# Turning the last tile of an attention unit on TensorE instead of by DMA

## Chip, cores and metric

The kernel runs on one core of a Trainium2 chip. The metric is the time of one execution in device microseconds; profiles come from single executions.

## What is computed

An attention with a learned bias on relative positions, then two feed-forward layers, each two matrix products with a function between them. Cut to what matters:

```python
B, H, S, D = 2, 8, 576, 64                       # q, k, v: (B, H, S, D)
scores = q @ k.transpose(0, 1, 3, 2) / np.sqrt(D)
x = log1p(abs(i - j)) / log1p(max(i, 1))         # one number for each pair of positions
bias = relu(x[..., None] @ w1 + b1) @ w2         # 32 hidden, one output for each head
attn = softmax(scores + bias)
y = (attn @ v).transpose(0, 2, 1, 3).reshape(1152, 512)
h = y @ moe_w_in                                 # (1152, 512) x (512, 2048)
g = (a0 + a1*h + a2*h**2 + a3*h**3) / (1 + abs(b0)*abs(h) + abs(b1)*h**2 + 1e-6)
y = g @ moe_w_out                                # (1152, 2048) x (2048, 512)
out = leaky_relu(y @ moe2_w_in, 0.01) @ moe2_w_out
```

## The kernel before

Four stages follow each other in one program. The engines' queues are in order, and the order in each is written out by hand: lists of pairs (step, operation) say at which step of a loop an operation is issued, and within a step the order of the list holds.

**Bias** (to about 76 us): the bias of all pairs is built and laid into `bias_m` and `bias_r` in SBUF.

**Attention** (about 76 to 237 us): a unit is a pair of heads of one batch entry; there are 8 units. A unit has 9 tiles of 128 rows x 576 columns: tiles 0 to 7 are four row blocks of either head, and the ninth (j = 8, tile (8, 2)) holds the last 64 rows of both heads. Step s of the loop belongs to tile s (9 steps a unit). For a tile:

- `qk` (L721): scores on TensorE in fp32r, six matmuls, issued one step ahead. Their PSUM pool has two buffers.
- `ttr` (L733): VectorE adds the bias and takes the row minimum, out of PSUM into `pt`.
- `exps` (L749): ScalarE takes the exponent into one of two `ex` buffers and sums the rows into `sums`.
- `hi`, one step later (L771 on ScalarE, L773 on VectorE, by the sets `HI_ACT`): the exponent is cast to fp16, first half of the buffer `hl`.
- `lo`, two steps later (L786): what the cast lost is put into the second half of `hl`. The first 512 columns go to GpSimd or, by `LO_DVE`, to VectorE; the last 64 to VectorE or, by `REM_POOL`, to GpSimd. The sets with `_END` hold for the last unit.
- When a group of tiles is complete in `hl` (two tiles, or the ninth alone: `GROUPS`), SyncE issues a DMA transpose into `et` (L792), where the columns lie on partitions. `hl` has three buffers.

Behind a unit come, by `PLAN` (steps count from the unit's first tile, so that step 9 is step 0 of the next unit): `rsum`, `rrec` (L819, L823: one over the row sums), `rbx` (L829, a product with the identity turns them; L832 copies it), `rbc` (L840, L842: spread over partitions), `av` with c = 0, 1, 2 (L813: attention times v, fp16, 28 matmuls each; c = 2 is the ninth tile), `rev` (L846), `rmul` (L855), `xhi`, `xlo` (L859, L864: the result split in two fp32r halves). Ahead of a unit come `load`, `prep_q`, `prep_ql`, `prep_k`, `v_sum`, `v_scale`, `prep_v8`, `prep_vd`. The outputs of `av` and of `rbx`/`rbc` share one PSUM tag, "v", with two buffers; `v_sum` and `v_scale` use spare columns of `rbc`'s.

`TAIL` is the same for the last two units (its first argument is 0 for the unit before the last, 1 for the last). In between stand the first operations of the next stage: the first weights (`w_load`, `w_dve`, `w_hi`, `w_lo`), the first product `gemm1` (L359, one call is nine matmuls of 384 columns, or three for one chunk) and the function on its result (`r_abs`, `r_s1` and so on). The first ones of `START` follow.

**First and second feed-forward layer** (to the end): products L359, L940 and L981 on TensorE, the rational function on VectorE, ScalarE and GpSimd (`plan_first` arranges the first layer, `PLAN2` the second).

Of the kernel before, what the change touches and what calls it, by code (L numbers as in the profile page):

```python
# [156 lines left out]
TAIL = [(2, 'rbx', 0), (3, 'rbc', 0), (2, 'w_load', -2, 0), (1, 'av', 0, 0, 0, 1), (0, 'rsum', 0),
        (0, 'rrec', 0), (8, 'w_dve', -2, 1, 0, 1), (18, 'w_lo', -2, 1), (7, 'av', 0, 1, 0, 1),
        (6, 'rmul', 0, 0), (5, 'w_dve', -2, 0, 0, 1), (8, 'w_load', -2, 1), (9, 'rsum', 1),
        (9, 'rrec', 1), (12, 'xhi', 0, 1), (12, 'open_h0'), (10, 'rbx', 1), (12, 'w_dve', -2, 1, 1, 2),  # L160
        (14, 'av', 1, 1, 0, 1), (7, 'av', 0, 2, 0, 1), (9, 'rmul', 0, 1), (9, 'w_dve', -2, 2, 0, 1),
        (11, 'w_dve', -2, 0, 1, 2), (12, 'rbc', 1), (9, 'xhi', 0, 0), (9, 'av', 1, 0, 0, 1),
        (10, 'w_hi', -2, 0), (21, 'w_dve', -1, 0, 1, 2), (15, 'av', 1, 2, 0, 1), (11, 'w_lo', -2, 0),
        (12, 'gemm1', 0, 0), (12, 'rev', 1), (12, 'rmul', 1, 0), (3, 'rev', 0),
        (12, 'w_dve', -2, 2, 1, 2), (14, 'w_load', -1, 0), (15, 'w_hi', -2, 1), (13, 'gemm1', 0, 2),
        (15, 'gemm1', 0, 3, (0,)), (16, 'w_dve', -1, 0, 0, 1), (21, 'w_hi', -1, 0), (21, 'r_s1', 0, 2),
# [1038 lines left out]
```

## Time and profile before

| | |
|---|---|
| median of 3 runs | 674.03 us (673.1 to 675.94) |
| profiled execution | 678.19 us, span of its instructions 676.4 us |
| TensorE busy | 598.4 us, 88% of the span |
| VectorE busy | 526.1 us, 78% |
| ScalarE busy | 410.2 us, 61% |
| GpSimd busy | 360.0 us, 53% |
| granted TensorE clock, mean | 0.959 |

All times of instructions are counted from the span's start. [...]

### The profile page before, as it was taken

What the parts mean: (1) busy time and instruction counts of PE and PEld (TensorE: products, weight loads), DVE (VectorE), ACT (ScalarE), POOL (GpSimd) and SP (SyncE); (2) the same over time, 40 slices, a digit from 0 to 9 for tenths busy, and PEclk for the clock granted to TensorE, in tenths of its full rate; (3) what the DMA queues carried; (4) which work ended last, traced back from release to release, by engine and by line L of the source; (5) the groups of instructions that cost most, each with busy time, mean ns of one, the idle gap of its engine ahead of it and who ended that gap; (6) DMA issues with size and microseconds to landing.
All of it is one profiled execution on the core that took longest, in us unless ns stands there. A gap on an engine that the chain in (4) does not pass through costs nothing.

```text
span 676.4 us, 11799 instructions
## 1 busy us (share of the span) xinstructions
PE 598.4 (88%) x4595; PEld 528.8 (78%) x4595; DVE 526.1 (78%) x809; ACT 410.2 (61%) x625; POOL 360.0 (53%) x263
## 2 busy tenths in 40 slices
PE   5767778889888866779999998999999999999998
PEld 3333557778677856779998898999999999999876
DVE  7999889988979577888999999998256465645463
ACT  9999678888868357687687686754254223232210
POOL 5766687766756412467547565752154634453340
PEclk9998979998979788879999999999999999999999
DMA  5666799999969812113122211011132313230113
GB/s 191 185 165 189 214 158 205 210 189 194 160 127 175 192 62 89 67 63 125 62 71 71 108 63 63 31 64 63 48 112 91 125 63 111 76 125 31 60 50 125
DMA packets 102199, 77.35 MB, mean 114 GB/s; under 512 B 86400, under 2 KB 86784, under 8 KB 102144
## 3 DMA queue, kind: packets, MB, share of 16 engines
q1 hardware_dynamic: 100848, 68.97, 40.0%
q10 hardware_dynamic: 1296, 7.64, 3.5%
q8 instruction: 36, 0.59, 0.3%
q14 instruction: 19, 0.16, 0.1%
HBM read 42.39 MB, written 2.36 MB: 66 GB/s over the span
## 4 chain that ended last, share of the span: by engine, by line
PE 50%; DVE 25%; ACT 6%; issue 5%; DMA 3%; POOL 1%; SPq 0%; DVEq 0%; ACTq 0%; POOLq 0%
PE ph L359 20%; PE pz L981 13%; PE py L940 7%; PE ps L721 5%; DVE raw L320 2%; DVE ph L412 2%; DVE raw L318 2%; PE pv L813 2%; DVE raw L316 2%; DVE bias L952 2%; DMA biasr<-in_moe_w_in 2%; DVE s L433 2%; DVE s L436 2%; DVE pt L733 2%; DVE qq L403 1%
## 5 line engine op out<-in xcount | busy, mean ns | idle before, releaser
L359 PE MATMUL ph<-bias,bias 128*128 128x384 f32 x1152 | 218.5, 345 | 15.4 <-DVE s L433 12.8
L359 PEld LDWEIGHTS ph<-bias,bias 128*128 128x128 f32 x1152 | 209.5, 195 | 20.8 <-issue 12.8
L786 POOL TENSOR_TENSOR hl<-ex,hl 128x512 f16<-128x512 f32 (+2 forms) x94 | 91.5, 991 | 38.1 <-DVE hl L773 20.7
L454 POOL TENSOR_TENSOR gl<-s,gh 128x1152 fp32r<-128x1152 f32 (+1 forms) x33 | 85.5, 2595 | 35.6 <-ACT gh L449 35.1
L721 PE MATMUL ps<-kt,qz 128*128 128x288 f32 x432 | 80.9, 328 | 21.5 <-DVE mn L733 16.2
L721 PEld LDWEIGHTS ps<-kt,qz 128*128 128x128 f32 x432 | 64.6, 203 | 33.7 <-DVE mn L733 17.6
L338 POOL TENSOR_TENSOR bias<-raw,bias 128x512 fp32r<-128x512 f32 x37 | 49.1, 1329 | 74.9 <-ACT bias L330 74.9
L940 PE MATMUL py<-gh,wo 128*128 128x384 f32 x288 | 80.7, 340 | 4.0 <-DVE bias L952 3.4
L989 DVE TENSOR_TENSOR bias<-pz,bias 128x512 f32<-128x512 f32 x48 | 33.1, 689 | 59.8 <-PE pz L981 59.5
L981 PE MATMUL pz<-wo,gh 128*128 128x512 f32 (+1 forms) x240 | 74.4, 386 | 0.3 <-DVE bias L989 0.3
L338 POOL TENSOR_TENSOR wo<-raw,wo 128x512 fp32r<-128x512 f32 x23 | 30.3, 1318 | 78.1 <-ACT wo L330 78.0
L749 ACT ACTIVATE ex<-pt,mn 128x576 f32<-128x576 f32 x72 | 55.3, 768 | 19.0 <-DVE mn L733 15.3
L629 PEld LDWEIGHTS <-coef 128*32 128x32 f16 x1152 | 27.3, 99 | 41.9 <-issue 27.4
L647 POOL TENSOR_TENSOR t<-t,te 128x576 f32<-128x576 f32 x36 | 47.0, 1310 | 22.4 <-DVE bb L652 12.9
L940 PEld LDWEIGHTS py<-gh,wo 128*128 128x128 f32 x288 | 52.6, 188 | 8.1 <-DVE bias L952 6.2
L733 DVE CUSTOM_DVE_ANT_0 pt<-ps,bias 128x576 f32<-128x576 f32 x64 | 47.4, 744 | 6.7 <-PE ps L721 5.4
L330 ACT ACTIVATE wo<-raw 128x512 fp32r<-128x512 f32 x27 | 17.0, 629 | 58.1 <-DVE raw L320 58.1
L940 PE MATMUL py<-gl,wo 128*128 128x384 f32 x156 | 52.2, 335 | 0.0
L441 ACT ACTIVATE s<-ph 128x1152 f32<-128x1152 f32 x16 | 18.2, 1136 | 54.8 <-PE ph L359 43.5
L981 PEld LDWEIGHTS pz<-wo,gh 128*128 128x128 f32 x240 | 44.3, 188 | 8.2 <-DVE bias L989 0.7
L981 PE MATMUL pz<-wo,gl 128*128 128x512 f32 (+1 forms) x129 | 50.1, 389 | 0.0
L430 POOL TENSOR_TENSOR qq<-qq,r 128x1152 f32<-128x1152 f32 (+1 forms) x15 | 37.9, 2524 | 16.6 <-ACT r L419 12.0
(134 smaller groups left out, 1188.9 us busy)
## 6 DMA issues: line engine op xcount, KB each, us to landing
biasr<-in_moe_w_in SPq DMA_DIRECT2D x32, 512.0 KB, 4.4
biasr<-in_moe_w_out SPq DMA_DIRECT2D x32, 512.0 KB, 3.5
...
et<-hl SPq DMA_TRANSPOSE x40, 4.8
...
```

The costliest lines, as they stand in the source:

```text
L338: G.tensor_tensor(lo_, raw[:, x], hi_.bitcast(F32), ALU.subtract)
L359: PE.matmul(ps[:, c, 0:CH], w[:, sl], x[kk][:, c * CH:(c + 1) * CH], start=(kk == 0 and n == 0), stop=(kk == KD - 1 and n == 2),)
L430: G.tensor_tensor(part(qq[f], c), part(qq[f], c), part(r0[f], c), ALU.mult)
L454: eng.tensor_tensor(part(gl, c), part(s1[f], c), part(gh, c).bitcast(F32), ALU.subtract)
L647: G.tensor_tensor(t1, t0s.pop(n), te[:, S - first_row(n):2 * S - first_row(n)], ALU.mult)
L721: PE.matmul(ps[:, c, 0:288], lt[:, a], kts[i][:, b, 288 * c:288 * c + 288], start=(n == 0), stop=(n == 2),)
L733: V.tensor_tensor_reduce(out=c2(pt), in0=s_ps.pop((i, j))[:, :, 0:288], in1=c2(bsrc), op0=ALU.add, op1=ALU.min, scale=1.0, scalar=3.0e38, ...
L749: A.activation(et, pt, AF.Exp, bias=mn, scale=-1.0, accum_out=sums[i][:, col:col + 1],)
L786: engines[j in at].tensor_tensor(hl[:, xs, dst], e9[:, xs, src], hl[:, xs, src], ALU.subtract)
L940: PE.matmul(ps[:, 0:CH], w[:, sl], gts[f][x][:, cs], start=(f == f0 and m == 0), stop=(f == f0 + nf - 1 and m == 2),)
L981: PE.matmul(ps[:, half], gts[f][x][:, sl], w[:, half], start=(f == f0 and m == 0), stop=(f == f0 + nf - 1 and m == 2),)
L989: V.tensor_tensor(dst, ps[:, half], dst, ALU.add)
```

## The change

The ninth tile of a unit is no longer cast, subtracted and turned by DMA. `hi` and `lo` return at once for j = 8. Instead, `flip` multiplies the fp32 exponents with the identity on TensorE, in a buffer of the PSUM tag "v": four blocks of 128 columns, and the last 64 columns twice, on either half of the partitions. `flip_hi` (ScalarE) copies 640 columns out of PSUM as fp16 into `et`; `flip_lo` (VectorE) subtracts them from PSUM and writes the second parts, in two instructions. `PLAN` has flip at step 9 and the other two at step 10; rbx goes from step 11 to 12, xhi from 22 to 23. `TAIL` has the three for both of its units, and some operations in other places. The sets that share out casts and subtractions in the last unit change, and two entries of `START` change places.

```diff
-PLAN = [(-24, 'load'), (14, 'rbc'), (17, 'av', 2, 0, 1), (22, 'xhi'), (-2, 'prep_k'), (18, 'rmul'),
-        (16, 'av', 1, 0, 1), (1, 'prep_v8'), (-3, 'v_scale'), (17, 'rev'), (11, 'rbx'), (-4, 'v_sum'),
-        (12, 'av', 0, 0, 1), (10, 'rrec'), (-1, 'prep_ql', 1), (2, 'prep_vd'), (27, 'xlo'),
-        (-4, 'prep_q', 0), (9, 'rsum'), (-2, 'prep_q', 1), (-3, 'prep_ql', 0)]
+PLAN = [(-3, 'v_scale'), (10, 'flip_hi'), (10, 'flip_lo'), (-24, 'load'), (14, 'rbc'),
+        (17, 'av', 2, 0, 1), (23, 'xhi'), (-2, 'prep_k'), (18, 'rmul'), (16, 'av', 1, 0, 1),
+        (1, 'prep_v8'), (12, 'rbx'), (-4, 'v_sum'), (12, 'av', 0, 0, 1), (10, 'rrec'), (17, 'rev'),
+        (-1, 'prep_ql', 1), (2, 'prep_vd'), (27, 'xlo'), (-4, 'prep_q', 0), (9, 'flip'), (9, 'rsum'),
+        (-2, 'prep_q', 1), (-3, 'prep_ql', 0)]
...
+TAIL = [(0, 'flip', 0), (1, 'flip_hi', 0), (1, 'flip_lo', 0), (7, 'av', 0, 1, 0, 1),
+        (10, 'flip_hi', 1), (10, 'flip_lo', 1), (2, 'rbx', 0), (3, 'rbc', 0), (2, 'w_load', -2, 0),
...
+        (18, 'w_lo', -2, 1), (9, 'flip', 1), (6, 'rmul', 0, 0), (5, 'w_dve', -2, 0, 0, 1),
+        (12, 'xhi', 0, 1), (8, 'w_load', -2, 1), (9, 'rsum', 1), (9, 'rrec', 1), (12, 'open_h0'),
...
-        (10, 'w_hi', -2, 0), (21, 'w_dve', -1, 0, 1, 2), (15, 'av', 1, 2, 0, 1), (11, 'w_lo', -2, 0),
+        (9, 'xhi', 0, 0), (9, 'av', 1, 0, 0, 1), (11, 'w_hi', -2, 0), (21, 'w_dve', -1, 0, 1, 2),
...
-        (15, 'gemm1', 0, 3, (0,)), (16, 'w_dve', -1, 0, 0, 1), (21, 'w_hi', -1, 0), (21, 'r_s1', 0, 2),
+        (15, 'w_hi', -2, 1), (13, 'gemm1', 0, 2), (14, 'gemm1', 0, 3, (0,)),
...
-START = [('split_hi', 0, 0), ('gemm1', 1, 0), ('split_lo', 0, (0,), 0), ('gemm1', 1, 1),
+START = [('gemm1', 1, 0), ('split_hi', 0, 0), ('split_lo', 0, (0,), 0), ('gemm1', 1, 1),
...
-REM_POOL_END = (1, 7, 8)
+REM_POOL_END = (1, 5, 6, 7)
...
-HI_ACT_END = (0, 1, 4, 5, 6, 7, 8)
-LO_DVE_END = (0, 5)
-HI_ACT = (1, 3, 5, 7, 8)
+HI_ACT_END = (0, 2, 4, 5, 6, 7, 8)
+LO_DVE_END = (0, 2, 5, 6, 7, 8)
+HI_ACT = (1, 3, 5, 7)
...
+        def flip(i):
+            ps = psv.tile(SHP, F32, tag="v", name="tp").rearrange("p c n -> p (c n)")
+            src = s_pt.pop((i, 8))[:, 0]
+            for b in range(4):
+                PE.matmul(ps[:, 128 * b:128 * b + 128], src[:, 128 * b:128 * b + 128], ident, start=True, stop=True)
+            for e in range(2):
+                PE.matmul(ps[64 * e:64 * e + 64, 512:640], src[:, 512:S], ident, start=True, stop=True)
+            pvs["t", i] = ps
+
+        def flip_hi(i):
+            A.activation(ets[i][:, 8, 0:5].rearrange("p k q -> p (k q)"), pvs["t", i][:, 0:640], AF.Copy)
+
+        def flip_lo(i):
+            ps, et = pvs.pop(("t", i)), ets[i][:, 8].rearrange("p k q -> p (k q)")
+            V.tensor_tensor(et[:, 640:1152], ps[:, 0:512], et[:, 0:512], ALU.subtract)
+            V.tensor_tensor(et[64:128, 512:640], ps[64:128, 512:640], et[64:128, 512:640], ALU.subtract)
+
         def hi(i, j):
+            if j == 8:
+                return
...
         def lo(i, j):
+            if j == 8:
+                return
```

## Rows read from the trace of the kernel before

**Rows 1.** Windows: units 2, 4, 5, 6, last tiles, end, rest; busy us (instructions), clock, DMA.

```profile
113.39:129.42 16.03, 14.71 (x156) 12.43 (x156) 14.51 (x34) 13.78 (x30) 11.70 (x13) 1.00 1.05 196
148.24:167.20 18.96, 16.58 (x164) 14.00 (x160) 15.72 (x35) 15.10 (x33) 12.85 (x14) 0.91 0.98 178
167.20:186.68 19.48, 15.86 (x167) 13.47 (x163) 17.98 (x35) 16.35 (x35) 14.80 (x15) 1.00 0.90 157
186.68:205.38 18.70, 17.30 (x156) 14.29 (x156) 14.87 (x36) 13.74 (x30) 11.36 (x13) 0.82 0.77 129
205.38:219.84 14.46, 12.39 (x116) 10.69 (x114) 13.13 (x31) 12.46 (x27) 8.40 (x9) 1.00 0.92 187
219.84:237.34 17.50, 15.47 (x168) 14.10 (x162) 10.21 (x19) 5.95 (x14) 7.75 (x7) 0.80 0.84 186
258.51:676.40 417.89, 395.42 (x2086) 370.77 (x2085) 303.59 (x348) 207.16 (x239) 201.59 (x108) 0.98 0.23 79
```

**Rows 2.** Timeline of VectorE in unit 4: start, us, instruction, idle before it.

```profile
150.26 1.13 DVE L819 TENSOR_SCALAR r<-sums,vsc 128x9 f32<-128x9 f32 x1
...
158.85 0.76 DVE L733 CUSTOM_DVE_ANT_0 pt<-ps,bias 128x576 f32<-128x576 f32 x1 [1.89 <-PE ps L721]
```

**Rows 3.** Timeline of GpSimd in unit 4.

```profile
149.84 1.78 POOL L786 TENSOR_TENSOR hl<-ex,hl 128x512 f16<-128x512 f32 x2 [0.33 <-POOL hl L786]
```

**Rows 4.** Groups by shape, 130 to 290 us; last two rows: lines L819, L786, min/median/max.

```profile
L786 POOL TENSOR_TENSOR hl<-ex,hl 128x512 f16<-128x512 f32 x37 | 48.9, 1322 | 24.5 <-DVE hl L773 11.1 <-issue 5.1 <-ACT hl L771 3.4
L786 DVE TENSOR_TENSOR hl<-ex,hl 128x512 f16<-128x512 f32 x10 | 8.8, 884 | 0.0
L846 ACT ACTIVATE rs<-pr 128x576 f32<-128x576 f32 x6 | 3.8, 638 | 2.4 <-PE pr L842 2.4
L855 DVE TENSOR_TENSOR xx<-pv,rs 128x576 f32<-128x576 f32 x5 | 3.8, 754 | 0.0
...
L819 DVE TENSOR_SCALAR r<-sums,vsc x8: 220/863/1127, 95.3 to 223.3; 128x9 f32<-128x9 f32 x8
L786 DVE TENSOR_TENSOR hl<-ex,hl x34: 212/681/1477, 84.6 to 220.5; 128x512 f16<-128x512 f32 x16, 128x64 f16<-128x64 f32 x10, 128x128 f16<-128x128 f32 x8
```

**Rows 5.** Timeline of TensorE in units 3 and 4.

```profile
144.58 1.72 PE L813 MATMUL pv<-et,vs 128*64 128x256 f16 x28
...
148.22 1.90 PE L721 MATMUL ps<-kt,qz 128*128 128x288 f32 x12
152.10 1.06 PE L721 MATMUL ps<-kt,qz 128*128 128x288 f32 x6 [1.98 <-DVE mn L733]
...
154.82 2.88 PE L813 MATMUL pv<-et,vs 128*64 128x256 f16 x28
...
159.44 1.15 PE L840 MATMUL pr<-rt,sm 9*128 9x128 f32 x8
```

**Rows 6.** Waits, 76 to 228 us: who for whom, us in total, times, longest.

```profile
PE ps L721 <- DVE mn L733: 16.2, 23, 2.0
DVE pt L733 <- PE ps L721: 5.4, 4, 1.9
DVE hl L773 <- DMA et<-hl: 1.9, 2, 1.7
```

**Rows 7.** Timeline of ScalarE, then the chain that ended last, around the end.

```profile
221.12 0.76 ACT L749 ACTIVATE ex<-pt,mn 128x576 f32<-128x576 f32 x1
...
227.26 7.23 PE ph L359 x27
234.49 2.09 PE pv L813 x56
...
239.32 2.32 PE ph L359 x6
...
320.33 6.24 PE ph L359 x36
```

**Rows 8.** Line L792: transposes on SP's queue, ns min/median/max.

```profile
L792 SPq DMA_TRANSPOSE et<-hl x40: 1286/2740/5936, 84.3 to 227.3; - x40
```

More of the change, by code (lines that the diff above doesn't have):

```diff
@@ L152 @@
 EXP_FIRST = False
-PLAN = [(-24, 'load'), (14, 'rbc'), (17, 'av', 2, 0, 1), (22, 'xhi'), (-2, 'prep_k'), (18, 'rmul'),
-        (16, 'av', 1, 0, 1), (1, 'prep_v8'), (-3, 'v_scale'), (17, 'rev'), (11, 'rbx'), (-4, 'v_sum'),
-        (12, 'av', 0, 0, 1), (10, 'rrec'), (-1, 'prep_ql', 1), (2, 'prep_vd'), (27, 'xlo'),
-        (-4, 'prep_q', 0), (9, 'rsum'), (-2, 'prep_q', 1), (-3, 'prep_ql', 0)]
[L157 to L162, printed above, removed]
-        (10, 'w_hi', -2, 0), (21, 'w_dve', -1, 0, 1, 2), (15, 'av', 1, 2, 0, 1), (11, 'w_lo', -2, 0),
-        (12, 'gemm1', 0, 0), (12, 'rev', 1), (12, 'rmul', 1, 0), (3, 'rev', 0),
-        (12, 'w_dve', -2, 2, 1, 2), (14, 'w_load', -1, 0), (15, 'w_hi', -2, 1), (13, 'gemm1', 0, 2),
-        (15, 'gemm1', 0, 3, (0,)), (16, 'w_dve', -1, 0, 0, 1), (21, 'w_hi', -1, 0), (21, 'r_s1', 0, 2),
@@ new lines @@
+PLAN = [(-3, 'v_scale'), (10, 'flip_hi'), (10, 'flip_lo'), (-24, 'load'), (14, 'rbc'),
[5 more added lines that the diff above has]
+        (10, 'flip_hi', 1), (10, 'flip_lo', 1), (2, 'rbx', 0), (3, 'rbc', 0), (2, 'w_load', -2, 0),
+        (1, 'av', 0, 0, 0, 1), (0, 'rsum', 0), (0, 'rrec', 0), (8, 'w_dve', -2, 1, 0, 1),
+        (18, 'w_lo', -2, 1), (9, 'flip', 1), (6, 'rmul', 0, 0), (5, 'w_dve', -2, 0, 0, 1),
+        (12, 'xhi', 0, 1), (8, 'w_load', -2, 1), (9, 'rsum', 1), (9, 'rrec', 1), (12, 'open_h0'),
+        (10, 'rbx', 1), (12, 'w_dve', -2, 1, 1, 2), (14, 'av', 1, 1, 0, 1), (7, 'av', 0, 2, 0, 1),
+        (9, 'rmul', 0, 1), (9, 'w_dve', -2, 2, 0, 1), (11, 'w_dve', -2, 0, 1, 2), (12, 'rbc', 1),
+        (9, 'xhi', 0, 0), (9, 'av', 1, 0, 0, 1), (11, 'w_hi', -2, 0), (21, 'w_dve', -1, 0, 1, 2),
+        (15, 'av', 1, 2, 0, 1), (11, 'w_lo', -2, 0), (12, 'gemm1', 0, 0), (12, 'rev', 1),
+        (12, 'rmul', 1, 0), (3, 'rev', 0), (12, 'w_dve', -2, 2, 1, 2), (14, 'w_load', -1, 0),
+        (15, 'w_hi', -2, 1), (13, 'gemm1', 0, 2), (14, 'gemm1', 0, 3, (0,)),
+        (16, 'w_dve', -1, 0, 0, 1), (21, 'w_hi', -1, 0), (21, 'r_s1', 0, 2),
@@ L178 @@
         (22, 'w_hi', -1, 1), (23, 'r_q1', 0, 1), (21, 'r_h3', 0, 1), (23, 'r_e', 0, 1),
-        (24, 'r_v', 0, 2), (24, 'r_v', 0, 1), (24, 'r_fin', 0, 2), (23, 'w_load', 0),
-        (24, 'r_fin', 0, 1)]
-START = [('split_hi', 0, 0), ('gemm1', 1, 0), ('split_lo', 0, (0,), 0), ('gemm1', 1, 1),
+        (24, 'r_v', 0, 2), (24, 'r_v', 0, 1), (23, 'w_load', 0), (24, 'r_fin', 0, 1),
+        (24, 'r_fin', 0, 2)]
+START = [('gemm1', 1, 0), ('split_hi', 0, 0), ('split_lo', 0, (0,), 0), ('gemm1', 1, 1),
          ('split_hi', 0, 2), ('gemm1', 1, 2), ('split_hi', 0, 1), ('gemm1', 1, 3), ('g2', 1, 0),
@@ L871, in attn_bias_moe_kernel @@
             for f in (load, prep_v8, prep_vd, prep_q, prep_ql, prep_k)
-            + (av, rsum, rrec, rbx, rbc, rev, rmul, xhi, xlo)
+            + (av, rsum, rrec, rbx, rbc, rev, rmul, xhi, xlo, flip, flip_hi, flip_lo)
         }
@@ L876, in attn_bias_moe_kernel @@
         ops["v_scale"] = lambda i: v_scale(i, prs[i - 2][:, 640:768])
-        post = {"av", "rsum", "rrec", "rbx", "rbc", "rev", "rmul", "xhi", "xlo"}
+        post = {"av", "rsum", "rrec", "rbx", "rbc", "rev", "rmul", "xhi", "xlo", "flip", "flip_hi", "flip_lo"}
         def open_h0():
```

## The prediction

> **What bounds the kernel now.** I read the page first, for the engines' shares and where TensorE's clock is down; then a table of windows cut at the starts of the units; then the timelines of one unit, the groups of instructions by shape, the waits, and last the chain that ended last around the end of the attention. The change touches units 0 to 7, so what comes after about 258 us (417.9 us, [rows 1]) can only be shifted by it.
>
> In the table the units from the second to the sixth take 16.0 to 19.5 us, 18.4 in the mean (92.0 us from 113.39 to 205.38, [rows 1]). In the four of them shown no engine is full: VectorE is busy 14.5 to 18.0 us of a unit, TensorE 14.7 to 17.3, ScalarE 13.7 to 16.4, GpSimd 11.4 to 14.8 [rows 1]. The unit is a loop between in-order queues, and VectorE, which opens each tile (the add-and-minimum of L733), is nearest to setting it. Unit 4 shows the pattern. The tiny L819 stands 1.13 us on VectorE, from 150.26 to 151.39 [rows 2], while GpSimd is on the low parts of the last tile, from 149.84 to 151.62 [rows 3]; in eight units its median is 0.86 us, at its shortest it is 0.22 [rows 4]. TensorE has no scores to start until 152.10 and idles 1.98 us [rows 5]. The clock granted in that unit is 0.91 [rows 1]; the 28 attention-times-v products at 154.82 take 2.88 us where the same 28 at 144.58 took 1.72 [rows 5], and VectorE then waits 1.89 us for scores [rows 2]. Such waits of L733 for scores come to 5.4 us, 4 times [rows 6]. The other wait to note: the fp16 buffer `hl`, for which VectorE casts waited 1.9 us in all until a DMA transpose had landed, 1.7 of it at once [rows 6].
>
> At the end, after the last L733 (219.84), a chain of products counts: 27 matmuls of the first expert weight take 7.23 us, then 56 of L813, then 6 more matmuls 2.32 us [rows 7]; later 36 of the same kind take 6.24 us [rows 7]. The granted clock of the first of these stretches is 0.80, that of the long rest 0.98 [rows 1].
>
> **The change, part by part.**
>
> *Turn by TensorE (flip), at step 9, which is step 0 of the next unit.* Four blocks of 128 columns and two of 64 by the identity, all fp32. The nearest row is the fp32 product of L840, four blocks in 1.15 us [rows 5], 0.29 a block, so 1.70 us for six. [...] Cover: in unit 4 the flip can start when the scores of tile 1 are done, about 149.2 (half of the 12 matmuls at 148.22, [rows 5]), and ends at 150.9, the next scores at 151.8; those after them waited until 152.10 anyway. So the idle 1.98 us hides it. With that cover gone (as in the second unit, 16.03 us) it costs 1.70 us: bounds 0 to 1.7 a unit.
>
> *flip_hi, ScalarE.* 128x640 out of PSUM, against 0.638 us for 576 [rows 4]: 0.70 us. It replaces a cast of 576 columns on the same engine, so ScalarE pays 0 to 0.1, one step later in its queue. Behind it stand `prep_v8` and the exponent of tile 1; that exponent needs its L733, which in unit 4 ends at about 152.1, when the last of the two is over: covered. Without that cover the exponent comes up to 0.7 us later.
>
> *flip_lo, VectorE.* 128x512 out of PSUM: 0.754 us for 576 [rows 4] gives 0.68. A piece of 64 partitions x 128: the shortest instruction of L786 on VectorE, 64 columns, took 0.212 [rows 4], the 512 above 0.68; it is nearest to the first, I take 0.25. Sum 0.93 us a unit, 5.6 in the six. It waits for flip_hi, and behind it in VectorE's queue stands L733 of tile 2, on which scores and exponents hang. In unit 4 the flip ends at 150.9, flip_hi at 151.6, and VectorE, without 0.9 us of L819, gets there at 151.5: 0.1 us. In a unit where L819 was short already it stands up to 1.5 us. I take 0.3 a unit, 1.8 in the six; bounds 0 and 9.0.
>
> *Removed from GpSimd:* two operations a unit for the last tile, 1.78 us [rows 3], 1.32 of it in the mean for the 512 columns [rows 4]. It is not the bound; what counts is what stood behind it: L819 goes from 0.86 to 0.22, 0.64 us a unit, -3.8 us in the six. Other end: 0, if another GpSimd operation slides there.
>
> *Removed from the DMA queue:* 8 of 40 transposes, the single ones, at 1.29 us of SP's queue each, the shortest of their line [rows 8]. The gain is the wait for `hl`, because its three buffers now carry four groups a unit, not five: -1.7 us; bounds 0 and -1.9 [rows 6].
>
> *Clock.* If the flip fills TensorE's idle, the dips in the units lose what stood before them in unit 4, and nearly all of the 5.4 us in which L733 waited for scores goes: -5.2; bounds 0 and -5.4.
>
> Six units: 5.6 + 1.8 - 3.8 - 1.7 - 5.2 = -3.3 us.
>
> *Sets of the last unit.* Three subtractions of 512 columns (tiles 2, 6, 7) go from GpSimd to VectorE, the remainders of two tiles go to GpSimd, two casts change places (0). The same subtraction on VectorE means 0.884 us, median of all of its shapes 0.681 [rows 4]. [...] Remainders: -2 x 0.25. With flip_lo 0.93 and L819 -0.64: +2.4 us of VectorE, in a stretch where it has 1.3 us idle (14.46 less 13.13, [rows 1]). I take +1.7, half of that idle used; bounds 0 and +2.7.
>
> *Around the end.* Flip, flip_hi and flip_lo of unit 7 now precede its rbx, for both want one of the two `v` buffers: exponent done at 221.9 [rows 7], flip 223.6, flip_hi 224.4, flip_lo 225.3, the product of tiles 0 and 1 in the gap. About 0.9 us for rbx and its copy and 1.7 for rbc (six blocks again) put the 27 matmuls at 228.0, 0.7 us later than 227.26 [rows 7]. But at full clock they take 27 x 6.24 / 36 = 4.68 us, -2.55. Chunk 0's last product goes ahead of the 28 small matmuls of L813, 2.09 for 56 [rows 7] less 1.72 for the 28 large ones, -0.4. Sum -2.25; bounds +0.7 and -3.5 (the six at 239.32 at full clock as well, 1.3 us).
>
> *Rest* (REM_POOL_END, START, one step more for rbx, xhi, w_hi): moves on engines that wait there; 0, or some tenths either way. xhi's cover is ScalarE's waits for L733; without it, an exponent comes 0.67 us later.
>
> Whole: -3.3 + 1.7 - 2.25 = -3.85 us on the profiled execution's 678.19 us (span 676.4). That execution is 4.2 us above the median of the runs, and I carry the difference over: 674.03 - 3.85 = **670.2 us**.
>
> **Rivals.**
>
> 1. *VectorE pays and stands: slower.* flip_lo stands in an in-order queue behind TensorE and ScalarE. If the flip is reached late (no idle to hide in), every unit pays 0.93 + 1.5 us: 14.6 - 3.8 - 1.7 = +9.1, +1.7 in the last unit: 684.8. It decides, past 3.4 us slower, where flip_lo waits over 1.5 us in the mean unit with the dips gone, or over 0.2 with the dips kept. For it: the second unit ran in 16.03 with VectorE and TensorE close behind each other. Against: TensorE's waits for L733 come to 16.2 us, 23 times [rows 6], 2 us a unit.
>
> 2. *The clock falls all the same.* Unit 5 ran at 1.00 and yet took 19.48 us [rows 1], so dips are not the only thing, and they may come at other places: without -5.2 and -2.55 the sum is +3.9: 677.9; with the units' part kept 672.7, with the end's part kept 675.4.
>
> 3. *More than the sum.* Less GpSimd work also shortens other casts and subtractions on VectorE that stood in its way (unit 5: VectorE busy 17.98, unit 6 14.87, [rows 1]), and all units come near 17.3 us, where TensorE's work ends: 15.3 at full clock (14.71 and 15.86 in units 2 and 5, [rows 1]) + 1.7. That is -1.1 us a unit, -6.6, and -3 at the end: 664.4.
>
> 4. *Hidden anyway:* casts, transposes and flip all lie beside other work, 674.
>
> **How the numbers follow.** A measurement of this kernel tells about 0.5%, 3.4 us, from no change: faster is below 670.7, slower above 677.4. Forecast (667 to 673) 0.40; rival 3 (660 to 667) 0.18; rivals 2 and 4 together 0.25; rival 1 0.17. Faster: rival 3 and most of the forecast, 0.35: 0.53. Slower: rival 1 but for its lower edge, and the upper edge of rival 2: 0.17. Within: 0.30. The range leaves out one in ten on either side: 663 to 678.
>
> **What would show it.** Right: SP issues 32 transposes; TensorE has a group of 1.7 us in its former idle stretch; no dip of the granted clock between 130 and 200 us and none before the 27 matmuls; L819 at 0.22; waits of L733 for scores under 2 us; units near 18 us, the second longer than 16. Wrong: flip_lo behind idle time of over 1 us, ended by ScalarE, in most units; dips elsewhere; the stretch from the last L733 to the first r_abs (17.5 us, [rows 1]) not under 16.5; or a changed length of the 417.9 us that I took as fixed.

## The result, and the profile after

The changed kernel takes 683.21 us (median of 4 runs, 677.91 to 685.18); the kernel before, run beside it, 674.99. The ratio is 1.0122 (95% interval 1.0076 to 1.0168): slower, where 0.6% faster was forecast. The profiled execution took 683.17 us, its span 681.4 against 676.4. So the two profiles differ by 5.0 us, the medians of the runs by 8.2: the profiled execution of the kernel before (678.19 us) was a long one, and the loss that the profiles show is the smaller for it. One execution of e1 (1134.96 us) and one of e9 (689.5) were in a slower state and are left out of the numbers below.

Windows of the changed kernel's profile, cut as in [rows 1] at the first turn of scores of each unit (units 1 to 6, then last tiles, end, rest); columns as there:

```profile
94.62:113.19 18.57, 18.18 (x168) 15.91 (x168) 14.56 (x36) 13.80 (x30) 9.90 (x11) 0.84 0.97 161
113.19:132.77 19.58, 17.00 (x179) 14.56 (x175) 16.52 (x37) 15.75 (x34) 12.50 (x13) 1.00 0.94 185
132.77:152.58 19.81, 16.74 (x171) 14.08 (x171) 18.02 (x37) 15.19 (x32) 11.61 (x12) 1.00 0.78 167
152.58:171.39 18.81, 16.73 (x171) 14.09 (x171) 16.99 (x37) 15.18 (x32) 10.62 (x11) 1.00 0.83 160
171.39:191.21 19.82, 16.73 (x171) 14.07 (x171) 18.02 (x38) 15.19 (x32) 12.76 (x13) 1.00 0.72 135
191.21:211.03 19.82, 16.77 (x171) 14.09 (x171) 18.01 (x37) 15.19 (x32) 11.66 (x12) 1.00 0.63 121
211.03:226.85 15.82, 14.02 (x110) 12.29 (x112) 14.76 (x32) 11.91 (x25) 5.67 (x6) 0.89 0.68 140
226.85:242.24 15.39, 13.97 (x166) 12.31 (x164) 9.97 (x21) 5.89 (x14) 3.48 (x4) 1.00 0.89 187
263.50:681.40 417.90, 395.15 (x2086) 370.62 (x2085) 304.02 (x348) 206.73 (x239) 201.53 (x108) 0.98 0.23 79
```

The six units take 116.4 us (94.62 to 211.03), before 110.75 (94.63 to 205.38): +5.7. The last tiles take 15.82 against 14.46, +1.4; the end 15.39 against 17.50, -2.1; the rest 417.90 against 417.89 [rows 1]. So the loss lies in the six units, at a granted clock of 1.00 in five of them. Units 3, 5 and 6 have settled on 19.8 us, and VectorE is busy for 18.0 of each.

VectorE's own account of the six units is in the sums of their windows, first before, then after:

```profile
sum 110.75, PE 98.03 PEld 82.66 DVE 95.03 ACT 88.37 POOL 75.76; mean PE 16.34 PEld 13.78 DVE 15.84 ACT 14.73 POOL 12.63
```

```profile
sum 116.41, PE 102.16 PEld 86.82 DVE 102.12 ACT 90.29 POOL 69.06; mean PE 17.03 PEld 14.47 DVE 17.02 ACT 15.05 POOL 11.51
```

It is busy for 7.1 us more and idle for 1.4 less. Of the 7.1, flip_lo is 5.9 (0.98 us, six times). The other 1.2 are instructions that "stand", that is, take longer than the shortest of their kind, in the rows shown beside a GpSimd instruction that began before them: L819's standing is gone, 3.1 us in the six units of before (four of its six took 0.60 to 1.13 us, two 0.22), and others have grown by some 4.3.

What was to show the steps right is mostly there. TensorE's timeline at the start of unit 3 has the flip at its place, but behind a wait for `prep_ql`:

```profile
132.79 0.55 PE L724 MATMUL ps<-kt,qz 128*128 128x288 f32 x2 [1.15 <-DVE qz L490]
133.18 1.05 PE L769 MATMUL tp<-sm,ex 128*128 128x128 f32 x8
134.16 0.44 PE L771 MATMUL tp<-sm,ex 128*64 128x128 f32 x4
```

Groups of the changed kernel around the flip, then two of its lines with minimum, median and maximum, and two waits (76 to 228 us):

```profile
L775 ACT ACTIVATE et<-tp 128x640 f16<-128x640 f32 x8 | 5.6, 701 | 4.0 <-PE tp L771 3.6
L779 DVE TENSOR_TENSOR et<-tp,et 128x512 f16<-128x512 f32 x8 | 5.5, 687 | 2.9 <-ACT et L775 2.9
L780 DVE TENSOR_TENSOR et<-tp,et 64x128 f16<-64x128 f32 x8 | 2.4, 295 | 0.1
```

```profile
L843 DVE TENSOR_SCALAR r<-sums,vsc x8: 221/227/228, 95.3 to 230.1; 128x9 f32<-128x9 f32 x8
L816 SPq DMA_TRANSPOSE et<-hl x32: 2461/2760/5155, 84.2 to 231.2; - x32
```

```profile
DVE pt L736 <- PE ps L724: 3.4, 6, 0.8
POOL hl L810 <- DMA et<-hl: 0.2, 1, 0.2
```

flip_lo waited 2.9 us for flip_hi in all, 2.2 of it in the six units; `rsum` (L843, before L819) takes 0.22 us every time; SyncE issues 32 transposes; no VectorE cast waits for one any more; VectorE's waits for scores went from 5.4 us [rows 6] to 3.4. And the units are longer. VectorE's timeline at the end of unit 3 and at the end of unit 4:

```profile
147.85 1.63 DVE L795 CAST hl<-ex 128x576 f16<-128x576 f32 x1
...
150.95 1.60 DVE L490 SCALAR_TENSOR_TENSOR qz<-qkv,qz 64x576 fp32r<-64x576 f32 x1
...
170.60 0.76 DVE L490 SCALAR_TENSOR_TENSOR qz<-qkv,qz 64x576 fp32r<-64x576 f32 x1
```

and GpSimd's beside it:

```profile
147.75 1.42 POOL L498 TENSOR_TENSOR kt<-qkv,kt 128x576 fp32r<-128x576 f32 x1 [1.11 <-ACT kt L497]
...
150.33 1.61 POOL L810 TENSOR_TENSOR hl<-ex,hl 128x512 f16<-128x512 f32 x1
...
170.71 1.68 POOL L810 TENSOR_TENSOR hl<-ex,hl 128x512 f16<-128x512 f32 x1
```

The cast of tile 6 (L795), 0.45 us at its shortest, begins 0.1 us after GpSimd's low half of k (L498) and takes 1.63: it ends 0.3 us after GpSimd is done. It takes 1.63 to 1.69 us in units 2 to 6. In the kernel before, in unit 4, the same cast came 0.28 us ahead of the low half of k and took 0.46:

```profile
164.10 0.46 DVE L773 CAST hl<-ex 128x576 f16<-128x576 f32 x1
```

```profile
164.38 1.46 POOL L495 TENSOR_TENSOR kt<-qkv,kt 128x576 fp32r<-128x576 f32 x1 [1.63 <-ACT kt L494]
```

But it stood there too, in unit 1 (1.39 us) and in unit 5, behind the low half of k that GpSimd had begun at 181.84:

```profile
181.99 1.59 DVE L773 CAST hl<-ex 128x576 f16<-128x576 f32 x1
```

`prep_ql` took 1.61 us at that unit's end, and the unit is the one of 19.48 us with VectorE busy for 17.98 [rows 1], at a clock of 1.00: nearly the settled unit of the changed kernel. What the kernel before met in two units of six, the changed one meets in five.

`prep_ql` (L490), the low half of q for the next unit, takes 1.60 at the end of unit 3, where it begins 0.6 us behind GpSimd's subtraction of 512 columns, and 0.76 at the end of unit 4, where it begins 0.1 us ahead of it. TensorE's first scores of the next unit wait for it:

```profile
PE ps L724 <- DVE qz L490: 4.0, 4, 1.3
```

(132.7 to 211 us). Unit 4 is the one of 18.81 us. In unit 3 the cast and `prep_ql` end 0.3 and 0.6 us after the GpSimd instruction that began before them. The first instruction of flip_lo, with one of its inputs in PSUM, took 0.69 us in unit 2, where it began (116.29) while GpSimd was subtracting (115.88 to 117.05), and 0.683 to 0.692 in all eight units.

### The profile page after: what moved, and what is told of

Its sections match the earlier page's. It is cut to its first block, busy times and chain, and to the rows that moved or that the text cites. A ratio compares the mean times of both kernels' runs of the same rounds, so it can differ in the third digit from the quotient of the medians.

```text
span 681.4 us, 11954 instructions
## 1 busy us (share of the span) xinstructions
PE 603.9 (89%) x4691; PEld 533.4 (78%) x4691; DVE 535.4 (79%) x826; ACT 410.2 (60%) x625; POOL 346.3 (51%) x246
## 4 chain that ended last, share of the span: by engine, by line
PE 39%; DVE 20%; ACT 4%; issue 3%; DMA 1%; POOL 1%; SPq 0%; DVEq 0%; ACTq 0%; POOLq 0%
PE ph L362 18%; PE pz L1005 13%; PE py L964 7%; DVE raw L323 2%; DVE raw L321 2%; DVE ph L415 2%; DVE raw L319 2%; DVE bias L976 2%; DVE s L436 2%; DVE s L412 2%; DVE s L439 1%; DVE qq L406 1%; ACT s L402 1%; DMA biasr<-in_moe_w_in 1%; ACT gh L452 1%
## 5 line engine op out<-in xcount | busy, mean ns | idle before, releaser
L362 PE MATMUL ph<-bias,bias 128*128 128x384 f32 x1152 | 215.1, 341 | 15.5 <-DVE s L436 13.0
L362 PEld LDWEIGHTS ph<-bias,bias 128*128 128x128 f32 x1152 | 205.7, 192 | 21.2 <-issue 13.2
L810 POOL TENSOR_TENSOR hl<-ex,hl 128x512 f16<-128x512 f32 (+2 forms) x77 | 78.0, 1029 | 55.8 <-DVE hl L795 33.1
L724 PEld LDWEIGHTS ps<-kt,qz 128*128 128x128 f32 x432 | 63.8, 200 | 34.2 <-DVE mn L736 16.2
```

Source lines behind the costliest of these rows:

```text
L362: PE.matmul(ps[:, c, 0:CH], w[:, sl], x[kk][:, c * CH:(c + 1) * CH], start=(kk == 0 and n == 0), stop=(kk == KD - 1 and n == 2),)
L724: PE.matmul(ps[:, c, 0:288], lt[:, a], kts[i][:, b, 288 * c:288 * c + 288], start=(n == 0), stop=(n == 2),)
L810: engines[j in at].tensor_tensor(hl[:, xs, dst], e9[:, xs, src], hl[:, xs, src], ALU.subtract)
```

## The experiments

Ratios are to the kernel before, run on the same chip; "six units" is from the profile, as above (before 110.7, changed 116.4). One profile is one execution: those of e2, e6, e9 and e18 are of the lowest run of their kernel.

| run | median us | ratio (95%) | six units |
|---|---|---|---|
| e1_old_places | 682.80 | 1.0102 (1.0027 to 1.0177) | 115.1 |
| e2_cast_act | 680.44 | 1.0117 (1.0069 to 1.0164) | 111.5 |
| e3_double_flip | 688.19 | 1.0222 (1.0181 to 1.0262) | 119.1 |
| e5_flip_last | 674.75 | 1.0003 (0.9971 to 1.0035) | 109.2 |
| e4_lo_act | 675.66 | 1.0028 (1.0007 to 1.0049) | 108.4 |
| e6_prep_k | 675.04 | 1.0021 (0.9998 to 1.0043) | 109.6 |
| e7_before_cast_act | 674.47 | 1.0023 (0.9992 to 1.0055) | 109.8 |
| e8_flip_last_old_sets | 674.19 | 1.0016 (0.9993 to 1.0038) | 109.1 |
| e9_before_prep_k | 684.70 | 1.0146 (1.0099 to 1.0193) | 118.3 |
| e10_before_both | 674.40 | 1.0012 (0.9987 to 1.0038) | 111.9 |
| e11_prep_k_cast_act | 677.20 | 1.0049 (1.0029 to 1.0069) | 110.3 |
| e12_prep_ql | 685.59 | 1.0174 (1.0142 to 1.0205) | 118.9 |
| e13_prep_k_bf16 | 679.93 | 1.0102 (1.0068 to 1.0136) | 115.0 |
| e14_bf16 | 677.07 | 1.0044 (1.0018 to 1.0071) | 111.6 |
| e15_prep_k_double | 685.69 | 1.0174 (1.0140 to 1.0207) | 117.4 |
| e16_before_again | 674.52 | 1.0002 (0.9974 to 1.0029) | 110.0 |
| e17_v_red | 673.46 | 0.9992 (0.9974 to 1.0011) | 107.4 |
| e18_before_v_red | 676.19 | 1.0030 (1.0008 to 1.0053) | 107.2 |

### Which part of the change

> The changed kernel with the attention's side work back where it was (rbx at step 11, xhi at 22, the old order within a step); the turn by TensorE stays at steps 9 and 10. Theory 1 (VectorE's time: flip_lo itself, and VectorE instructions that stand behind GpSimd's): the units keep their length, six of them 115 to 118 us, the whole within 2 us of the changed kernel's 683. Theory 3 (the loss comes from the side work placed anew): six units back to 110 to 112 us, the whole near 676 to 678.

```diff
-PLAN = [(-3, 'v_scale'), (10, 'flip_hi'), (10, 'flip_lo'), (-24, 'load'), ...
+PLAN = [(10, 'flip_hi'), (10, 'flip_lo'), (9, 'flip'), ...  # then the list of the kernel before
```

682.80 us: within 0.5 of the changed kernel. The new places of the side work are not the cause.

> The turn by TensorE in the last unit alone; units 0 to 6 have the cast, the low part and the DMA transpose of their ninth tile, in the places of the kernel before; lists and sets of the last unit as changed. Theory 1: the loss lies in units 2 to 6 and the gain in the stretch from the last L733 to the first r_abs (15.4 us against 17.5), so six units as before (110 to 111 us), the last unit 14.5 to 16, the end 15 to 16, the whole 672 to 675. If the end's gain came from a clock that only the units' turns hold up, the end is 17 us or more and the whole 675 to 677.

```diff
-HI_ACT = (1, 3, 5, 7)
+HI_ACT = (1, 3, 5, 7, 8)
...
-            if j == 8:
+            if j == 8 and i == len(units) - 1:
```

(with `PLAN` of before). 674.75 us, the kernel before's time. The loss comes from units 0 to 6 alone, in the profile the end keeps its gain without them:

```profile
203.58:219.26 15.68, 13.29 (x98) 11.17 (x96) 14.75 (x31) 12.98 (x27) 8.85 (x10) 0.82 0.92 182
219.26:234.77 15.51, 14.95 (x174) 13.17 (x172) 11.15 (x20) 5.56 (x13) 3.21 (x4) 0.97 0.74 180
```

> The kernel before with TensorE's turn for the last unit's ninth tile alone, and with the kernel before's own division of the last unit's casts and remainders among the engines. Nothing is left out. If the 1.2 us that the last unit lost comes from the changed division (VectorE takes on a subtraction and a cast that GpSimd and ScalarE had): the last unit goes back to 14.5 to 14.9, the end keeps its 2.0, and the whole is 1 to 3 below the kernel before, 672 to 674. If it comes from the flip's own work in that unit: the last unit stays at 15.7 and the whole at 674 to 675.

```diff
-REM_POOL_END = (1, 5, 6, 7)
+REM_POOL_END = (1, 7, 8)
-HI_ACT_END = (0, 2, 4, 5, 6, 7, 8)
-LO_DVE_END = (0, 2, 5, 6, 7, 8)
+HI_ACT_END = (0, 1, 4, 5, 6, 7, 8)
+LO_DVE_END = (0, 5)
```

This is e5 with the last unit's old sets. Its windows of the last tiles and of the end:

```profile
204.10:218.55 14.45, 12.37 (x116) 10.69 (x114) 13.13 (x30) 12.25 (x27) 8.65 (x9) 1.00 0.92 187
218.55:235.69 17.14, 14.97 (x158) 12.93 (x154) 10.19 (x20) 5.86 (x13) 5.94 (x5) 0.90 0.73 172
```

The last tiles went back to 14.45, as expected, but the end went back too, to 17.14: the new sets lose 1.2 us in the one and give 1.6 back in the other. The two belong together; 31.2 us with the change and in e5, 31.6 here, 32.0 before.

### VectorE's work, or its standing

> The changed kernel with the fp16 cast of tile 6 on ScalarE instead of VectorE in units 0 to 6. Theory 1: in units 2 to 6 that cast took 1.63 us on VectorE because it stood behind GpSimd's low half of k; without it a unit is 1.2 to 1.6 us shorter, six units 107 to 110 us, the whole 674 to 677. If the standing only passes to the next VectorE instruction, the unit gains the cast's own 0.45 us, whole about 680. Theory 2 (TensorE's time sets the unit): no change, 683.

```diff
-HI_ACT = (1, 3, 5, 7)
+HI_ACT = (1, 3, 5, 6, 7)
```

In the profile the six units take 18.4 to 18.8 us each and the cast's standing is gone; but that execution was the lowest of five (676.78), and by the ratio the kernel gains next to nothing. Inconclusive.

> The changed kernel, with the two subtractions that write the low half of the last tile (0.685 and 0.295 us on VectorE, 0.98 a unit) replaced by one ScalarE copy with scale 0 into the 512 columns: the low half of the ninth tile is left out (zeros). VectorE's work is the only load taken off, ScalarE's rises by some 0.6 us a unit. Theory 1 (VectorE sets the unit, by its own time and by standing behind GpSimd): units 2 to 6 fall by at least the 0.98 that goes, 19.6 to 18.6 or less, and the whole to 674 to 677. Theory 2 (the way TensorE to ScalarE to VectorE, that is the wait for the flip, sets the unit): the way is as long as before, units stay at 19.6 and the whole within 1 of the changed kernel.

```diff
-            V.tensor_tensor(et[:, 640:1152], ps[:, 0:512], et[:, 0:512], ALU.subtract)
-            V.tensor_tensor(et[64:128, 512:640], ps[64:128, 512:640], et[64:128, 512:640], ALU.subtract)
+            A.activation(et[:, 640:1152], ps[:, 0:512], AF.Copy, scale=0.0)
```

675.66 us, as VectorE's time would have it: by the ratios 6.3 us less than the changed kernel (1.0122 less 1.0028, of 674), by the medians 7.5, about the 0.98 us in eight units. Yet its units 3 to 6 fall in two kinds, two of 16.9 and two of 18.6 and 19.1 us, all at a clock of 1.00, with VectorE busy for 15.24 us of either short one and for 16.89 and 17.25 of the long ones, units 3 and 5. The cast of tile 6 takes 1.57 us in unit 3, a long one, and 0.45 in unit 4, a short one:

```profile
145.49 1.57 DVE L794 CAST hl<-ex 128x576 f16<-128x576 f32 x1
```

```profile
163.94 0.45 DVE L794 CAST hl<-ex 128x576 f16<-128x576 f32 x1
```

So within one execution a standing cast goes with 1.7 us of unit (18.61 against 16.87).

> The changed kernel, with the preparation of the next unit's k taken one step earlier (step -3 in place of -2), so that GpSimd's low half of k does not run just ahead of VectorE's cast of tile 6. Nothing is left out. If the 1.2 us by which that cast stands longer (1.63 against 0.46) is what the unit lost: units 3 to 6 at 18.4 to 18.7 and the whole 676 to 679. If the standing only passes to another VectorE instruction behind the same GpSimd work: units unchanged at 19.8 or up to 0.5 either way, the whole 681 to 685.

```diff
-        (17, 'av', 2, 0, 1), (23, 'xhi'), (-2, 'prep_k'), (18, 'rmul'), (16, 'av', 1, 0, 1),
+        (17, 'av', 2, 0, 1), (23, 'xhi'), (-3, 'prep_k'), (18, 'rmul'), (16, 'av', 1, 0, 1),
```

One number, no work less: 675.04 us, by the ratios 6.8 us less than the changed kernel (1.0122 less 1.0021, of 674), by the medians 8.2. Windows of units 2 to 4, then the cast's and `prep_ql`'s rows on VectorE, then GpSimd's low half of k:

```profile
110.93:128.70 17.77, 16.21 (x171) 14.02 (x171) 14.70 (x37) 15.03 (x34) 11.39 (x12) 1.00 0.92 186
128.70:147.09 18.39, 16.46 (x171) 14.04 (x171) 16.02 (x38) 15.19 (x34) 11.29 (x12) 1.00 0.86 180
147.09:165.50 18.41, 16.48 (x171) 14.06 (x171) 16.02 (x38) 15.19 (x34) 11.27 (x12) 1.00 0.87 179
```

```profile
162.13 0.97 DVE L795 CAST hl<-ex 128x576 f16<-128x576 f32 x1 [0.52 <-issue]
...
164.71 0.76 DVE L490 SCALAR_TENSOR_TENSOR qz<-qkv,qz 64x576 fp32r<-64x576 f32 x1
```

```profile
161.37 1.42 POOL L498 TENSOR_TENSOR kt<-qkv,kt 128x576 fp32r<-128x576 f32 x1 [2.40 <-ACT kt L497]
```

The low half of k now begins 0.76 us ahead of the cast, not 0.1. The cast takes 0.97 instead of 1.63, `prep_ql` is short in all six units, and the settled unit is 18.4 us instead of 19.8. VectorE is busy for 93.6 us of the six units where it was 102.1 (14.86 in unit 1, then the rows above and two of 16.0; 223 and 222 instructions): 8.5 us of standing gone, and the six units are 6.9 shorter. Unit 0, ahead of them, is shorter too, 13.48 us for 15.59. And flip_lo is still there: with 7.3 us less standing than the kernel before (93.6 less 5.9, against 95.0), e6 is only level with it.

### The same step in the kernel before

> The kernel before, with the cast of tile 6 taken from VectorE to ScalarE, and no part of the change. If VectorE's time with its standing sets the units of the kernel before too: units 3 and 5 (18.96 and 19.48), where that cast or its neighbours stand, come down by 0.5 to 1 each, and the whole is 670 to 674. If the units of before are set by the arrival of the turned tile or by TensorE: 674 to 677, no change.

```diff
-HI_ACT = (1, 3, 5, 7, 8)
+HI_ACT = (1, 3, 5, 6, 7, 8)
```

No change: 674.47 us. The scores now wait for GpSimd's low half of k instead, 5.9 us in five units.

> The kernel before, with the preparation of the next unit's k one step earlier (-3 in place of -2) and nothing else; nothing is left out. In the kernel before TensorE's scores wait for VectorE's low half of q (1.3 us) in two of five units, 2.6 us in all, and for GpSimd's low half of k in five, 1.1 in all. Theory 1 (that chain sets the unit, and what was changed only shifts which units it strikes): both waits go, six units come down by 2 to 4 us, the whole to 669 to 672. Theory 2 (it strikes only with the flip in the unit, before's units being set by the turned tile and TensorE's 2 us waits): no change, 672.5 to 674.5.

```diff
-        ... (22, 'xhi'), (-2, 'prep_k'), (18, 'rmul'),
+        ... (22, 'xhi'), (-3, 'prep_k'), (18, 'rmul'),
```

Both theories missed. The step that gives the changed kernel 7 us costs the kernel before 10 by the ratio, 12.0 by the medians: 684.70. Its profile is of its lowest run (677.74): against the profile of before (678.19) the six units are 7.6 us longer, all the rest together 8.1 shorter. Line of `prep_ql`, minimum, median and maximum, from 94 to 212 us, in the kernel before, the changed kernel, e6 and e9, in this order:

```profile
L487 DVE SCALAR_TENSOR_TENSOR qz<-qkv,qz x13: 755/870/1609, 93.0 to 204.6; 64x576 fp32r<-64x576 f32 x13
```

```profile
L490 DVE SCALAR_TENSOR_TENSOR qz<-qkv,qz x13: 756/874/1608, 93.0 to 209.4; 64x576 fp32r<-64x576 f32 x13
```

```profile
L490 DVE SCALAR_TENSOR_TENSOR qz<-qkv,qz x12: 742/750/756, 105.6 to 201.5; 64x576 fp32r<-64x576 f32 x12
```

```profile
L487 DVE SCALAR_TENSOR_TENSOR qz<-qkv,qz x12: 756/1710/1740, 106.7 to 208.9; 64x576 fp32r<-64x576 f32 x12
```

In e6 none of the 12 stands (0.742 to 0.756 us), in e9 their median is 1.71 us. And in two of these units the granted clock fell to 0.83 (units 3 and 5 of e9):

```profile
131.48:151.82 20.34, 18.07 (x159) 14.93 (x159) 15.91 (x36) 14.10 (x31) 13.27 (x13) 0.83 0.77 166
...
171.63:191.69 20.06, 18.21 (x159) 15.01 (x159) 16.93 (x36) 15.18 (x33) 14.14 (x14) 0.83 0.81 122
```

> The kernel before, with k prepared one step earlier and the cast of tile 6 on ScalarE; nothing is left out. With the cast on ScalarE alone the scores waited 1.3 us for GpSimd's low half of k in each of five units, 5.9 in all. If that wait sets the unit there: units 18.1 to 17.0 to 17.4 and the whole 668 to 671. If another wait takes its place (VectorE's turn of the next scores): units stay at 18.1, the whole 673 to 675.

Both edits, e7's and e9's, in the kernel before: 674.40, as if nothing had been done; its units run from 16.2 to 21.6 us.

### Is it the wait for the low half of q, or TensorE

> The changed kernel, with VectorE's low half of the next unit's second q (0.76 us, up to 1.60 standing) one step earlier, ahead of the cast and of the scores' turns that it stood behind; k's preparation stays where it was. Nothing is left out. If the chain is: VectorE stands behind GpSimd, q's low half is late, TensorE's first scores wait 1.3 us for it (4 times in units 3 to 6): that wait goes with the cast's standing left in place, units 19.8 to 18.5 to 19.0 and the whole 676 to 679. If the standing itself costs its time wherever q's low half stands: units 19.4 to 19.8, the whole 681 to 684.

```diff
-        (-1, 'prep_ql', 1), (2, 'prep_vd'), ...
-        (-2, 'prep_q', 1), (-3, 'prep_ql', 0)]
+        (2, 'prep_vd'), ...
+        (-2, 'prep_q', 1), (-2, 'prep_ql', 1), (-3, 'prep_ql', 0)]
```

685.59: the wait of the scores for q went, the time did not. At its new place, in unit 4, `prep_ql` takes 1.37 us (168.70 to 170.07, with GpSimd busy for 1.96 of the 2 us from 168 to 170), and the subtraction after it takes 1.28. But the cast of that unit no longer stands (0.44 us), in units 5 and 6 VectorE is busy for 16.30 and 16.38 us and not 18.0, and still the two take 20.4 and 20.5, at a clock of 0.92. So it is not that one wait, and VectorE's standing is not all: less of it came with a lower clock and no shorter unit.

> The changed kernel, with k prepared one step earlier and the cast of tile 6 on ScalarE; nothing is left out. With k earlier alone, units stood at 18.4 with VectorE busy 16.0 and the scores' wait for q's low half down to 0.3 each. If VectorE's own time in the chain still sets the unit, 0.45 to 0.97 that the cast takes goes off: units 17.5 to 18.0, the whole 670 to 673. If TensorE (16.5 busy, 1.9 idle behind VectorE's turns of scores) or ScalarE (then some 16) sets it: units 18.2 to 18.6, the whole 674 to 677.

e2's and e6's edits together: the profile's settled unit is 18.40 us, exactly e6's, with VectorE busy 15.62 and not 16.02. VectorE's own work does not hold it there. The whole is no better, 677.20 us, by the ratios 1.9 more than e6.

> The changed kernel with the twelve matmuls of each turn issued twice (same result). Theory 1: TensorE has room in that stretch (it waited 1.26 us for VectorE right behind it), so 0 to 4 us more over all units, because part of the 1.5 us passes through flip_hi to flip_lo. Theory 2 (TensorE's time sets the unit): 1.5 us in each of eight units, 12 us more, 695.

```diff
-            for b in range(4):
+            for _ in range(2):
+                for b in range(4):
...
```

> The changed kernel with k prepared one step earlier and the flip's 12 matmuls made twice (TensorE 1.49 us more a unit); nothing is left out. If TensorE's stream holds the unit: 18.40 to 19.6 to 19.9, the whole 682 to 685. If it does not: units 18.4 to 18.8, the whole 675 to 678. In the changed kernel itself doubling gave units of 19.15.

The same doubling of the 12 matmuls on top of e6. In the changed kernel a second flip makes units 5 and 6 shorter, 19.15 us for 19.8 (VectorE busy 15.69), while unit 1 (21.95 for 18.57) and the last tiles (17.62 for 15.82) pay; the whole is 5 us longer, by the ratios 6.7. With k early the shortest of units 2 to 6 take 19.2 us, where e6's settled ones take 18.4: about half of the 1.49 us that the second flip takes. But two others take 20.07 and 20.25, the six together are 7.8 us longer than e6's, 1.3 a unit, and the whole goes to 685.69, just above where the theory of TensorE's stream had put it (682 to 685). A second flip is not free.

> The changed kernel with k prepared one step earlier, and the last tile turned from the upper 16 bits of each fp32 number, in bf16: the lower 16 bits of that tile are left out, and the 12 matmuls take about 1 us less (five bf16 ones of this size took 0.46 us on the chip, the fp32 ones 1.49 for 12). If TensorE's stream holds the unit at 18.40: units 17.2 to 17.6 and the whole 667 to 671. If the way over VectorE's turns of the scores holds it: units 18.2 to 18.4 and the whole 673.5 to 675.5.

```diff
-            src = s_pt.pop((i, 8))[:, 0]
+            up = lambda x: x.bitcast(BF16).rearrange("p (n y) -> p n y", y=2)[:, :, 1]
+            src, one = up(s_pt.pop((i, 8))[:, 0]), up(ident)
```

(and `one` for `ident`). A shorter flip makes the kernel slower, 679.93 against e6's 675.04. Windows of its units 3 to 5:

```profile
128.27:148.32 20.05, 15.70 (x165) 13.27 (x165) 16.91 (x37) 15.46 (x34) 12.28 (x14) 1.00 0.95 180
148.32:169.14 20.82, 19.78 (x165) 16.12 (x165) 15.85 (x37) 15.00 (x32) 9.72 (x9) 0.75 0.67 144
169.14:187.54 18.40, 15.64 (x165) 13.26 (x165) 15.90 (x37) 15.19 (x34) 11.28 (x12) 1.00 0.68 130
```

The third row is the settled unit again, 18.40 us, with TensorE busy 15.64 where e6 has 16.46: TensorE's flip time alone does not hold it either. Ahead of it stand units of 20 us, the second of them at a clock of 0.75.

> The changed kernel with the last tile turned from the upper 16 bits in bf16 as in the run with k earlier, k's preparation where the change has it: the lower 16 bits of that tile are left out. If the units of 19.8 are set by VectorE standing behind GpSimd (18.0 busy): they stay at 19.3 to 19.8, the whole 680 to 683. If TensorE's 1.49 us of flip is the added time: units 18.7 to 18.9 and the whole 675 to 677.

The same flip with k where the change has it: 677.07. That is the time the TensorE theory gave, but its units are not: 17.1, 17.2, 19.7, 19.3, 18.6, 19.8 us, the last again with VectorE busy 18.0. By the ratios it is 5.3 us less than the changed kernel. It does not decide between the theories, but it leaves the flip's time on TensorE as a possible part of the loss.

### What holds the unit of 18.4 us

> The changed kernel with k prepared one step earlier, and with VectorE's reduction of the sums over v one step later than TensorE's sums (it stood in the same step and waited 1.2 us a unit for them), the scale that ScalarE makes of it one step later too. Nothing is left out. If the chain from TensorE's sums over VectorE and ScalarE holds the unit at 18.40: units 17.2 to 17.7 and the whole 667 to 671. If it does not, or another standing takes its place: units 18.4 to 19.8 and the whole 675 to 683.

```diff
-PLAN = [(-3, 'v_scale'), ...                  # on top of e6
+PLAN = [(-3, 'v_red'), (-2, 'v_scale'), ...
...
+    def v_red(i, spare):      # VectorE's reduction, taken out of v_sum
         vd = opn.tile([128, 128], F32, name="vd", tag="vd", bufs=1)
         V.tensor_tensor_reduce(
```

673.46 us, the best of the kernels with the flip: 1.3% below the changed kernel by the ratios, and level with the kernel before. VectorE's wait of 1.2 us a unit for TensorE's sums is gone. Its units 3 to 6, and the two kinds of `prep_ql` at the ends of units 4 and 5:

```profile
128.27:147.07 18.80, 16.23 (x171) 14.02 (x171) 17.27 (x37) 15.19 (x32) 11.11 (x12) 1.00 0.84 175
147.07:165.88 18.81, 16.23 (x171) 14.01 (x171) 17.21 (x38) 15.20 (x32) 11.11 (x12) 1.00 0.93 167
165.88:182.99 17.11, 15.68 (x168) 13.69 (x169) 16.38 (x37) 14.33 (x31) 9.88 (x10) 1.00 0.68 132
182.99:200.02 17.03, 15.84 (x172) 13.84 (x171) 15.96 (x38) 14.90 (x33) 11.76 (x12) 1.00 0.74 140
```

```profile
164.24 1.61 DVE L490 SCALAR_TENSOR_TENSOR qz<-qkv,qz 64x576 fp32r<-64x576 f32 x1
...
182.21 0.76 DVE L490 SCALAR_TENSOR_TENSOR qz<-qkv,qz 64x576 fp32r<-64x576 f32 x1
```

Three of its units end with a `prep_ql` of 1.6 us and take 18.8 us; the two that follow end with one of 0.76 and take 17.1 and 17.0. Same program, same clock: one standing of 0.85 us goes with 1.7 us of unit.

> The kernel before with the same edit alone (VectorE's reduction of the sums over v and the scale each one step later). Nothing is left out. If that chain holds its units too: units of 18.6 to 19.5 come down by about 1, the whole 667 to 671. If a standing or the clock takes its place, as when k was moved there: 675 to 686.

The same edit in the kernel before: 676.19, no gain. Its profile (672.86, its lowest run) has units of 16.7 to 18.9.

> The kernel before, profiled once more. If its units repeat those of the first profile (16.0, 18.8, 19.0, 19.5, 18.7 for units 2 to 6), the first profile stands for it. If the kernel's units fall in patterns that differ from run to run, this profile has a span near the median of its runs, 671 to 673 where the first has 676.4, and another row of units: more of 16 to 17.5.

Units of 18.6, 17.9, 19.0, 19.5, 18.6 us for 2 to 6 (first profile: 16.0, 18.8, 19.0, 19.5, 18.7): nearly the same pattern; only the short unit comes first (16.4) and not second. Both profiled executions of the kernel before (678.19, 677.51) lie near the top of its runs (669.66 to 679.44). Why is left open.

## Why the prediction was wrong, point by point

**Costs of the new operations: right.** flip 1.49 us (8 matmuls 1.05, 4 of 64 columns 0.44) against 1.70; flip_hi 0.70 as forecast; flip_lo 0.98 against 0.93. flip_lo's waits for flip_hi, 1.8 us forecast in the six units, are 2.2.

**The reliefs happened, one by one.** L819 to 0.22 us, the wait for `hl` gone, no dip of the clock in units 2 to 6. One came short: the waits for scores fell from 5.4 us to 3.4, where under 2 was to show the step right.

**The step that failed: two of the three reliefs, taken in full as time off the units.** In the prediction's own terms VectorE's account of the six units reads: flip_lo +5.9 us (5.6 forecast), its waits +2.2 (1.8), the wait for `hl` -1.9 (-1.7), all three right. The waits for scores, which were to go with the dips, came to -2.0 instead of -5.2. And VectorE's standing, -3.8 forecast, came to +1.2. These two are 8.2 of the 9.0 us between -3.3 and the measured +5.7.

Of the standing the prediction gave the other end, "0, if another GpSimd operation slides there", and then took the full gain. That other end is what came, and worse: in the settled units the cast of tile 6 (1.63 us), `prep_ql` (1.60) and a remainder (0.77 against 0.25) stand behind GpSimd, 2.5 us a unit by their excess over the short form (1.7 in unit 4), where L819 had stood 0.64. The prediction did not ask which of VectorE's other instructions would meet which of GpSimd's.

That this standing costs time is shown by e6 (the same instructions, one step apart, are some 7 us shorter) and inside e4 (unit 4 takes 16.9 us with the short cast, unit 3 18.6 with the standing one). That it alone is the loss is not shown. The added work seems to count too: e4, which leaves out flip_lo's work, and e14, which shortens the flip, give back 6.3 and 5.3 us by the ratios, and e15 prices a further flip at 1.3 us a unit, a term that the sum had at 0. The runs do not part the shares. Why the small shift of the loop brings the cast behind k in five units instead of two is open as well.

**Rivals.** Rival 1 gave 684.8 us and is nearest in time. That is half luck: VectorE pays, as it said, but flip_lo was to wait 1.5 us a unit and waits 0.4, and other instructions stand instead. Rival 2 falls for units 2 to 6, where the clock was 1.00; but it pointed at unit 5 of the kernel before, long at full clock, and that was the unit to look into. Rival 3 said that less GpSimd work shortens the standing of other instructions; GpSimd's work did fall, by 6.7 us, and their standing grew. Its sum has a slip: 15.3 + 1.7 is 17.0 us and not 17.3, which would give some 662.6.

**Last unit and end: right together.** +1.4 and -2.1 us against +1.7 and -2.25. The forecast's +2.4 us of VectorE's time has three subtractions of 512 columns at the mean of their row, 0.884 us [rows 4], 2.65 together; no run shows that price in the last unit, where VectorE's five of that size took 0.68 to 0.79 each. At the end the 27 matmuls

```profile
234.85 4.98 PE L362 MATMUL ph<-bias,bias 128*128 128x384 f32 x27
```

began 8.0 us after the last turn of scores (226.85; before 7.4, [rows 1, 7]; 0.7 later was forecast) and took 4.98 us; 4.68 was forecast. e8 adds, in one profile, that the end's gain goes with the new sets of the last unit, which the prediction had booked to the clock and to the order alone.

**What the right phase is worth.** In e17, with VectorE busy for 98.0 us of them, the six units take 107.4 us, 3.3 less than in the profile of before. That it is the forecast number is chance, for the sum got there by other terms. Yet the medians of the two kernels are equal (0.9974 to 1.0011). The profiled execution was 4.2 us above the median, and carrying the whole difference over made 670.2 out of 674.3: the prediction's base was untypical of the runs, and so, it seems, were the waits that it meant to gain.

**Open:** what decides into which pattern a run falls, what holds the unit of 18.4 us, and whether some places of the side work make either kernel clearly faster; none of those tried did.
